# r of tiles 0 to 11 loaded in runs of eight tokens and turned by 64x64 transposes; rstd on ScalarE; a new order for all engines

## The chip, the cores and the metric

The kernel runs on one core of one Trainium2 chip. The engines of the core are TensorE (PE in the profile), VectorE (DVE), ScalarE (ACT), GpSimd (POOL) and SyncE (SP, which here only issues transfers). The metric is the device time of one execution in microseconds (us). The kernel before has a median of 148.78 us over three runs (147.83, 148.78 and 149.36).

## The reference

There are 4 batches, 8 heads, 768 tokens and 48 channels for each head. The first half is a linear recurrence of attention with a decay w for each head and channel, the second half is a feed-forward block on the 384 channels of a token.

```
state = 0                                            # per batch and head, 48 x 48
for t in range(768):
    cur = u * k[t] (outer) v[t]
    y[t] = r[t] @ (state + cur)
    state = w * state + k[t] (outer) v[t]

x  = y as (batch, token, 8 heads * 48 = 384)
xn = (x - mean(x)) / sqrt(var(x) + 1e-6) * g_ln
out = x + relu(xn @ w_ch1) @ w_ch2                   # 384 -> 1536 -> 384
```

All inputs and the output are in float32.

## The kernel before

**Tiles.** The 768 tokens of a batch are cut into 6 chunks of 128. A tile i is chunk i // 4 of batch i % 4, so there are 24 tiles of 128 tokens, and tile i needs the state that tile i - 4 leaves. Within a tile the recurrence becomes matrix products. With powers of w folded in, r is multiplied by w^t (`Fr`) and k by w^-(t+1) (`Fk`), t being the token's place in the chunk, which is its partition.

**Steps of one tile.** `LR`, `LK`, `LV` load r, k and v as [128 tokens, 8 heads, 48], so that every run in memory is 48 floats, 192 bytes. `SR` and `SK` scale r and k and write them in bf16 to `sc`, each head padded to 64 columns. `TR` turns r and k on TensorE with 128x128 transposes (line 348), two heads at a time, and `TCr`, `TCk` (or `TC` for both) copy the result from PSUM to `trs`. For tiles 12 to 23 (`K_BY_DMA`) a transposing transfer, `TKR`, does this instead. `AT` (line 371) makes the token-by-token products k r of all heads, from 48 rows of the array at row 0 or row 64; `AM` (or `AMa` and `AMb`) masks them into `A`. `Q` multiplies turned r and k; `S` sums that with u and w to the coefficient of a token's own v (line 402), copied by `CC` to `cc`, and makes the new state (lines 409 and 415), which `ZU` and `ZD` decay and keep as `Z`. `VB` forms cc * v, `Y` (lines 444 and 452) makes r state + A v, and `X` adds them to x and gives the row sum. `SQ` and `XN` centre x and sum its squares, `RS` makes the reciprocal of the standard deviation, `LT` (line 512) and `XT` turn the centred x, or `LT2` and `LTD` do so by a transfer.

**Feed-forward.** Tiles are taken in 17 groups of one or two (`GROUPS`). `UP` (line 527) multiplies by w_ch1 (12 matmuls of 128 or 6 of 256 columns), `RL` applies relu on the way out of PSUM, `DN` (line 557) multiplies by w_ch2 (4 matmuls of 384 columns), `OT` scales by `rs` and adds x, `STO` stores. For a group of one tile, `UP` number m needs third m of w_ch1. The weights come in thirds: `LW1` loads a third (768 KB), `SW` scales it by the layer norm's gain and rounds it to bf16 in three pieces; `LW2` and `CW` do the same for w_ch2. The last tile is finished in two halves (`DA`, `DB`, `OA`, `OB`, `SA`, `SB`).

**Order.** There is no planner in the kernel: the string `PLAN` lists some 800 steps as name, number and engine or PSUM bank ("v" VectorE, "s" ScalarE, "g" GpSimd; "h", "p", "o", "a" banks), and each step issues its instructions at once. Every engine works through its own instructions in that order, and a transfer marked "-" is issued by SP in that order too. `DU` issues matmuls on zeros while the first loads are under way.

The steps that matter most for what follows:

```
def chunk_src(t, i):
    c, b = divmod(i, B)
    return t[b, :, c * L : (c + 1) * L, :].rearrange("h t d -> t h d")
def LR(i, e):
    nc.sync.dma_start(out=rf(i)[:], in_=chunk_src(r, i))
def SR(i, e):
    times(e, scr(i)[:, :, :D], rf(i)[:], Fr[:])
```

Of the kernel before, what the change touches and what calls it, by code (L numbers as in the profile page):

```python
# [9 lines left out]
ALU = mybir.AluOpType  # L10
# [8 lines left out]
LR,1,- LK,0,- MI,0,g MW,0,v WF,0,s WB,0,- LC,0,s LC,1,s MM,0,g MP,0,v TL,0,s LC,2,s DU,21,h LN,0,s FK,0,s FR,0,s SK,0,v LK,1,- LR,0,- SK,1,v CT,0,o  # L19
DU,7,h SR,0,v TR,0,h TCk,0,s SR,1,v TR,1,h TCk,1,v TCr,0,s Q,0,v AT,0,- CP,0,s WL,0,s LR,2,- SR,2,g TCr,1,v LK,2,- SK,2,g TR,2,h AMb,0,v AMa,0,v  # L20
AT,1,- LV,1,- LK,3,- AMb,1,v AMa,1,v UW,0,g TCk,2,s TCr,2,s AT,2,- AMb,2,v UGC,0,s LV,0,- CV,0,s S,0,h CC,0,v VB,0,v ZU,0,v Y,0,h X,0,v XN,0,v LR,3,-
CV,1,s Q,1,g SK,3,g SR,3,g TR,3,- Q,2,g S,1,o CC,1,v VB,1,g ZU,1,v AMa,2,v Y,1,- X,1,v LK,5,- LR,4,- SR,4,g TCr,3,s TCk,3,s AT,3,- Q,3,v AM,3,v LV,2,-
CV,2,s S,2,h CC,2,s ZU,2,v LT,0,o XN,1,s XT,0,s LK,4,- LR,5,- SR,5,v VB,2,v SK,4,g DU,3,p TR,4,- TC,4,v Q,4,v LV,3,- CV,3,s S,3,o CC,3,s SQ,1,s ZU,3,v
LV,4,- SK,5,g TR,5,- TC,5,s VB,3,g Y,2,- X,2,v LT,1,- XT,1,s XN,2,s CV,4,g S,4,h ZU,4,v CC,4,s LV,5,- CV,5,g ATP,4,- AM,4,v LW1,0,- SW,1,s Y,3,h
SQ,0,s X,3,v XN,3,s SQ,2,s LT,2,h XT,2,v Q,5,g S,5,- AM,5,v ZU,5,v Y,4,o SW,2,g SW,0,g UP,16,- RL,16,s LW1,2,- SW,6,s CC,5,s LT,3,- XT,3,s UP,32,-
RL,32,s UP,0,- RL,0,s LW1,1,- SW,5,s VB,4,g X,4,v XN,4,v SW,7,g SW,8,g UP,2,o RL,2,v VB,5,g UP,48,p RL,48,v Y,5,h SW,3,g LK,6,- SK,6,v X,5,v UP,18,-
RL,18,s XN,5,s SW,4,g UP,49,p RL,49,s UP,33,o LR,7,- SR,7,v UP,34,- RL,34,s LK,7,- SK,7,g RS,2,g RL,33,v UP,17,- RL,17,s TR,7,p TC,7,s RS,0,g LT,5,h
XT,5,v LT,4,- UP,1,o LR,6,- Q,7,v LW2,2,- UP,82,- SR,6,g TR,6,- UP,81,- XT,4,s RL,1,v LV,7,- CV,7,v CW,5,v S,7,- CC,7,v ZU,7,v CW,4,g DN,6,- RL,82,v
TC,6,s Q,6,g ATP,6,- AM,7,v AM,6,v LW2,1,- CW,2,s SQ,4,s DN,2,p UP,50,- RL,50,s CW,3,g DN,5,- VB,7,g DN,1,- RL,81,v Y,7,h LW2,0,- CW,1,s CW,0,g DN,4,-
DN,0,- SQ,5,s RS,1,g OT,1,v LV,6,- CV,6,s S,6,h CC,6,s LK,9,- SK,9,g UP,66,o SQ,3,s X,7,v XN,7,g SQ,7,s VB,6,g ZU,6,v RL,66,v UP,64,- RL,64,s Y,6,h  # L30
LR,9,- SR,9,v LR,8,- SR,8,g DN,10,- RS,5,g TR,9,- X,6,v XN,6,s LK,8,- SK,8,v DN,8,- OT,0,v TR,8,- TC,8,v Q,8,v TC,9,s Q,9,v RS,3,g RS,4,g DN,9,-
OT,2,v UP,65,- RL,65,s ATP,8,- UP,80,p AM,9,v LV,9,- CV,9,g LR,10,- SR,10,g DN,18,- S,9,h ZU,9,v DN,17,- CC,9,v LK,10,- SK,10,g LV,8,- CV,8,s S,8,h
LR,11,- SR,11,v CC,8,v RL,80,s ZU,8,v VB,9,g TR,10,- AM,8,v TC,10,v VB,8,g LT2,6,- UP,96,- RL,96,s Q,10,v UP,98,p RL,98,s UP,97,- RL,97,s Y,9,h X,9,v
LK,11,- UP,100,p RL,100,s LV,10,- LR,15,- LK,12,- SK,11,g TR,11,- TC,11,s XN,9,v CV,10,g S,10,h Y,8,h X,8,v XN,8,s ZD,8,g DN,16,- ATP,10,- STO,0,-
OT,4,v UP,101,- RL,101,s UP,99,p LR,13,- SK,12,g SQ,6,s RL,99,s STO,1,- DN,22,- DN,20,- DN,21,- ZU,10,v AM,10,v DN,14,p CC,10,v DN,12,- Q,11,g ZD,10,v
SR,13,g LV,11,- CV,11,s S,11,h CC,11,s AM,11,v OT,5,v Y,10,h VB,10,v X,10,v ZD,9,g ZU,11,v LR,12,- SR,12,g LK,13,- SK,13,g LR,14,- SR,14,v VB,11,g
# [12 lines left out]
DN,49,- LV,19,- CV,19,s CC,18,s S,19,h ZU,19,v DN,42,- ZD,18,g VB,18,g STO,8,- OT,12,v CC,19,s Y,18,h X,18,v LT2,16,- UP,176,- RL,176,s LR,21,-
UP,178,o RL,178,s XN,18,s UP,181,- RL,181,s AM,19,v Y,19,h VB,19,v X,19,v XN,19,s DN,62,- DN,61,- DN,60,- LR,20,- STO,6,- OT,10,v LK,20,- LR,22,-  # L50
SR,22,v SQ,17,s DN,57,p UP,179,- RL,179,s RS,10,g UP,177,- RL,177,v STO,11,- DN,56,- UP,180,- SQ,16,s RL,180,s SR,21,g TKR,21,- Q,21,v OT,15,v DN,58,-
S,21,o CC,21,s LT2,18,- UP,194,- RL,194,s STO,10,- OT,14,v UP,196,- RL,196,v UP,192,p SK,20,g LK,22,- SK,22,v SQ,18,s UP,193,- RL,193,s UP,195,-
RL,195,s SR,20,g TKR,20,- Q,20,v ATP,20,- AM,20,v S,20,h DN,65,- DN,64,- ZD,19,g RL,192,s LV,20,- CV,20,s Y,20,h CC,20,v VB,20,v SQ,19,s X,20,v
# [11 lines left out]
def kernel(  # L65
# [262 lines left out]
    def LR(i, e):  # L328
        nc.sync.dma_start(out=rf(i)[:], in_=chunk_src(r, i))  # L329
# [333 lines left out]
```

## Time and profile before

| | |
|---|---|
| median of 3 runs | 148.78 us (147.83 to 149.36) |
| profiled execution: time, span from first to last instruction | 148.24 us, 146.5 us |
| mean granted TensorE clock | 0.965 |
| busy PE, DVE, ACT, POOL | 135.8, 110.5, 80.1, 94.0 us |
| DMA packets, and those under 512 bytes | 99267, 94508 |
| HBM read and written | 18.88 MB, 4.72 MB |

The busy times are sums over the whole span; they say little by themselves, since the span has a front in which the loads come in and the first tiles are prepared, a long middle in which the feed-forward runs, and an end. The rows of single stretches, the order of the instructions in time and the chain that ended last are shown where they are used.

### The profile page before, as it was taken

What the parts mean: (1) busy time and instruction counts of PE and PEld (TensorE: products, weight loads), DVE (VectorE), ACT (ScalarE), POOL (GpSimd) and SP (SyncE); (2) the same over time, 40 slices, a digit from 0 to 9 for tenths busy, and PEclk for the clock granted to TensorE, in tenths of its full rate; (3) what the DMA queues carried; (4) which work ended last, traced back from release to release, by engine and by line L of the source; (5) the groups of instructions that cost most, each with busy time, mean ns of one, the idle gap of its engine ahead of it and who ended that gap; (6) DMA issues with size and microseconds to landing.
All of it is one profiled execution on the core that took longest, in us unless ns stands there. A gap on an engine that the chain in (4) does not pass through costs nothing.

```text
span 146.5 us, 4250 instructions
## 1 busy us (share of the span) xinstructions
PE 135.8 (93%) x1693; PEld 108.2 (74%) x1693; DVE 110.5 (75%) x220; ACT 80.1 (55%) x175; POOL 94.0 (64%) x132
## 2 busy tenths in 40 slices
PE   3966699999999999999999999999999999999991
PEld 1455477998687897787688887966877777888871
DVE  4569999767969899985959948897946796875232
ACT  2575577977676467466386560663654752244600
POOL 4089878967888999989957493428553076644030
PEclk9999556999999999999999999999999999999999
DMA  5999899999889999899999999988999997830114
GB/s 97 209 211 221 175 277 401 194 258 380 231 170 188 206 197 232 156 215 242 96 229 206 260 233 186 217 166 185 245 157 199 229 184 156 206 123 0 54 37 182
DMA packets 99267, 28.59 MB, mean 195 GB/s; under 512 B 94508, under 2 KB 97712, under 8 KB 99248
## 3 DMA queue, kind: packets, MB, share of 16 engines
q1 hardware_dynamic: 98352, 27.24, 86.3%
q10 hardware_dynamic: 896, 1.09, 2.0%
q8 instruction: 13, 0.21, 0.6%
q14 instruction: 6, 0.05, 0.1%
HBM read 18.88 MB, written 4.72 MB: 161 GB/s over the span
## 4 chain that ended last, share of the span: by engine, by line
PE 60%; SPq 11%; DMA 11%; DVE 7%; POOL 6%; issue 4%; DVEq 0%; POOLq 0%
PE hp L527 17%; PE o L557 16%; PE s L557 7%; PE s L527 5%; SPq L332 4%; DMA w_f<-in_moe_w_ch_dram 4%; SPq L329 4%; SPq L326 3%; DMA trs<-sc 3%; DMA rf<-in_r_dram 3%; PE o L527 3%; PE at L371 2%; PE hp L452 2%; POOL sc L194 2%; PE at L348 2%
## 5 line engine op out<-in xcount | busy, mean ns | idle before, releaser
L527 PEld LDWEIGHTS <-w_sb 128*128 128x128 bf16 x612 | 47.9, 114 | 2.4 <-POOL w_sb L312 0.4
L527 PE MATMUL hp<-xT,w_sb 128*128 128x128 bf16 (+1 forms) x408 | 39.9, 244 | 0.3 <-POOL w_sb L312 0.3
L557 PEld LDWEIGHTS <-hT 128*128 128x128 bf16 x276 | 25.2, 97 | 13.7 <-issue 0.4
L557 PE MATMUL o<-w_sb,hT 128*128 128x384 bf16 x180 | 34.5, 326 | 0.0
L543 ACT ACTIVATE hT<-hp 128x512 bf16<-128x512 f32 x41 | 24.3, 597 | 18.2 <-PE hp L527 17.7
L381 DVE TENSOR_TENSOR A<-at,mask 128x1024 bf16<-128x1024 f32 (+1 forms) x27 | 28.9, 1096 | 1.2 <-PE at L371 1.2
L194 POOL TENSOR_TENSOR sc<-kf,Fk 128x384 bf16<-128x384 f32 x14 | 14.5, 1044 | 10.5 <-DMA kf<-in_k_dram 10.4
L434 POOL TENSOR_TENSOR Vb<-vf,cc 128x384 f32<-128x384 f32 x17 | 14.7, 868 | 8.7 <-ACT cc L189 3.6
L557 PE MATMUL s<-w_sb,hT 128*128 128x384 bf16 x96 | 18.9, 326 | 0.2 <-DVE x L459 0.2
L194 POOL TENSOR_TENSOR q<-trs 128x512 bf16<-128x512 bf16 x11 | 13.4, 1220 | 5.5 <-PE hp L527 2.6
L194 POOL TENSOR_TENSOR sc<-rf,Fr 128x384 bf16<-128x384 f32 x12 | 13.0, 1082 | 5.3 <-DMA rf<-in_r_dram 5.3
L466 ACT ACTIVATE sqj<-x,sm 128x384 bf16<-128x384 f32 x24 | 14.7, 611 | 1.4 <-DVE x L459 1.3
L615 DVE SCALAR_TENSOR_TENSOR ot<-o,rs,x 128x384 f32<-128x384 f32 x15 | 9.2, 613 | 4.5 <-POOL rs L483 2.8
L459 DVE SCALAR_TENSOR_TENSOR x<-hp,Vb 128x384 f32<-128x384 f32 x19 | 10.5, 554 | 2.3 <-PE hp L452 1.6
L483 POOL TENSOR_TENSOR rs<-rs,expo 128x1 f32<-128x1 f32 (+1 forms) x17 | 10.6, 625 | 1.4
L472 ACT ACTIVATE xn<-x,sm 128x384 bf16<-128x384 f32 x13 | 8.0, 613 | 5.7 <-DVE x L459 5.6
L371 PE MATMUL at<-trs 48*128 48x128 bf16 x192 | 8.6, 229 | 2.4 <-ACT trs L189 1.2
L527 PE MATMUL s<-xT,w_sb 128*128 128x128 bf16 (+1 forms) x120 | 10.8, 235 | 0.0
L194 POOL TENSOR_TENSOR Z<-ZS,WLZ 128x384 bf16<-128x384 f32 x10 | 10.3, 1030 | 0.6 <-DVE ZS L428 0.6
L545 DVE TENSOR_SCALAR hT<-hp 128x512 bf16<-128x512 f32 x9 | 6.2, 689 | 4.6 <-PE hp L527 4.6
L371 PEld LDWEIGHTS <-trs 48*128 48x128 bf16 x192 | 6.0, 99 | 4.9 <-ACT trs L189 2.1
L194 DVE TENSOR_TENSOR sc<-rf,Fr 128x384 bf16<-128x384 f32 x12 | 7.5, 633 | 2.3 <-DMA rf<-in_r_dram 2.2
(116 smaller groups left out, 214.3 us busy)
## 6 DMA issues: line engine op xcount, KB each, us to landing
rf<-in_r_dram SPq DMA_DIRECT2D x24, 192.0 KB, 3.8
kf<-in_k_dram SPq DMA_DIRECT2D x24, 192.0 KB, 3.9
vf<-in_v_dram SPq DMA_DIRECT2D x24, 192.0 KB, 3.9
w_f<-in_moe_w_ch_dram SPq DMA_DIRECT2D x6, 768.0 KB, 7.2
out_dram<-ot SPq DMA_DIRECT2D x18, 192.0 KB, 3.4
out_dram<-ot ACTq DMA_DIRECT2D x5, 192.0 KB, 2.0
trs<-sc SPq DMA_TRANSPOSE x12, 3.9
xT<-xn SPq DMA_TRANSPOSE x9, 2.8
```

What stands on the lines that cost most here:

```text
L194: engines[e].tensor_tensor(out=out, in0=in0, in1=in1, op=ALU.mult)
L371: nc.tensor.matmul(out=t[:, par, q, :], lhsT=trs(i)[p0 : p0 + D, 1, q, :], rhs=trs(i)[p0 : p0 + D, 0, q, :], start=True, stop=True,)
L381: nc.vector.tensor_tensor(out=AA(i)[:, a:b].rearrange("p e q t -> p (e q) t"), in0=psum["at", i][:, a:b].rearrange("p e q t -> p (e q) t") ...
L434: engines[e].tensor_tensor(out=Vb(i)[:].rearrange("p (h d) -> p h d", h=H), in0=vf(i)[:], in1=cc(i)[:].unsqueeze(2).to_broadcast([P, H, D] ...
L459: nc.vector.scalar_tensor_tensor(out=xx(i)[:], in0=psum["y", i][:, :C], scalar=1.0, in1=Vb(i)[:], op0=ALU.mult, op1=ALU.add, accum_out=sm[ ...
L466: nc.scalar.activation(out=sqj[:], in_=xx(i)[:], func=ACT.Square, bias=sm[i][:], scale=-float(C), accum_out=sq[g][:, j : j + 1])
L472: nc.scalar.activation(out=xn(i), in_=xx(i)[:], func=ACT.Identity, bias=sm[i][:], scale=-float(C))
L483: nc.gpsimd.tensor_tensor(out=rs[g][:], in0=rs[g][:], in1=expo[:, :n], op=ALU.pow)
L527: nc.tensor.matmul(out=t[:, a * gw : (a + 1) * gw].rearrange("p (j t) -> p j t", j=size), lhsT=w1_sb[n][kc][:, fb::FB], rhs=xT(g)[:, :size ...
L543: nc.scalar.activation(out=o, in_=s, func=ACT.Relu)
L557: nc.tensor.matmul(out=psum["o", i][:, :C], lhsT=hT(g)[:, fk, j * P : (j + 1) * P], rhs=w2_sb[d][:, a, :], start=(seen == 0 and a == 0), s ...
L615: nc.vector.scalar_tensor_tensor(out=ot(i), in0=psum["o", i][:, :C], scalar=rs[g][:, j : j + 1], in1=xx(i)[:], op0=ALU.mult, op1=ALU.add,)
```

## The change

**r of tiles 0 to 11.** `LR` no longer puts one token on each partition. Partition 16 h + p holds tokens 8 p to 8 p + 7 of head h, one run of 8 x 48 floats (1536 bytes). The power of w then depends on the head and on the place in the run, so there is a second table, `Fq`, with its own short preparation: `MR` and `MU` make the token numbers, `MS` a selection matrix, `WS` two matmuls that spread w over the partitions, `LNQ` their logarithm, `FA` the product, `FQ` the exponential. `Fr` is needed only from tile 12 on, is made later and shares its memory with the logarithms of `Fk`. `TR` turns r of these tiles with 16 transposes of 64x64 (eight places in the run, two halves of the partitions) in place of four of 128x128; k keeps its four. `TCr` writes the result with a stride of 8 so that tokens come in order. `TC`, which copied r and k together, is not used any more.

**Pairs of heads.** Since the lower half of the partitions now holds heads 0 to 3 and the upper half heads 4 to 7, the pairs of heads are (q, q + 4) and no longer (2q, 2q + 1). `SK`, `SR`, `CV`, `CC`, `LC` and `Y` put that order into their access patterns.

**rstd.** `RS` was two instructions on GpSimd, the second a power of -0.5. It is now a logarithm and an exponential on ScalarE, from the same activation table that the kernel loads already.

**VB** can also run on ScalarE, as 8 instructions of 48 columns; 3 of the 24 do.

**Order, engines and banks** are all set anew. Of the loads, the first third of w_ch1 now stands behind 18 loads of 192 KB, of which 7 are packed r, as before it stood behind 18 loads, all in runs of 192 bytes; the thirds of w_ch1 are no longer issued in a row, but with one k load, and then a k and an r load, between them. The steps before the first `UP` are nearly the same set: `S` of tile 5 and `Y` of tile 4 now come behind it.

```diff
+PACK = 8
+R_PACKED = 12
-... WB,0,- ... DU,21,h LN,0,s FK,0,s FR,0,s SK,0,v ... LV,3,- ... LV,4,- ... LV,5,- ... LW1,0,- SW,1,s ... LW1,2,- ... LW1,1,- ...
+LK,2,- LR,2,- LK,0,- MW,0,v MM,0,g WF,0,s LC,2,s WB,0,h LC,0,s TL,0,s MI,0,g MS,0,v WS,0,o LC,1,s LN,0,s MR,0,g MU,0,v MP,0,v FK,0,s SK,0,v DU,19,h
+LNQ,0,s FA,0,v FQ,0,s CT,0,o CP,0,s UGC,0,s UW,0,g SK,2,v LR,0,- SR,0,v TR,0,p TCr,0,s ...
+X,1,v ATP,4,- AM,5,v LW1,2,- SW,8,s SW,7,s XN,2,g LT,2,p XT,2,s XN,1,s SW,6,g UP,50,- RL,50,s LK,7,- SK,7,g LW1,0,- ...
...
-    expo = const.tile([P, GM], FP32, name="expo")
+    eps = const.tile([P, 1], FP32, name="eps")
-    ln_all = const.tile([P, H, D], FP32, name="ln_all")
+    ln_all = Fr
...
+    def WS(i, e):
+        t = psum["wq"] = bank(e, "p", [P, 512], FP32)
+        for a in range(2):
+            nc.tensor.matmul(
+                out=t[:, :D], lhsT=sel[:, 2 * a : 2 * a + 2, :].rearrange("k e x -> k (e x)"),
+                rhs=rows[:HP, a * DP : a * DP + D], start=(a == 0), stop=(a == 1),
+            )
+
+    def LNQ(i, e):
+        nc.scalar.activation(out=lnq[:], in_=psum["wq"][:, :D], func=ACT.Ln)
+
+    def FA(i, e):
+        times(
+            e, Fq[:], lnq[:].unsqueeze(1).to_broadcast([P, PACK, D]),
+            pow_r[:].unsqueeze(2).to_broadcast([P, PACK, D]),
+        )
+
+    def FQ(i, e):
+        nc.scalar.activation(out=Fq[:], in_=Fq[:], func=ACT.Exp)
...
     def LR(i, e):
-        nc.sync.dma_start(out=rf(i)[:], in_=chunk_src(r, i))
+        if i >= R_PACKED:
+            issuer(e).dma_start(out=rf(i)[:], in_=chunk_src(r, i))
+            return
+        c, b = divmod(i, B)
+        issuer(e).dma_start(
+            out=rf(i)[:].rearrange("p j d -> p (j d)"),
+            in_=r[b, :, c * L : (c + 1) * L, :].rearrange("h (p j) d -> h p (j d)", j=PACK),
+        )
...
     def SK(i, e):
-        times(e, sck(i)[:, :, :D], kf(i)[:], Fk[:])
+        times(e, paired(sck(i))[:, :, :, :D], plain(kf(i)[:]), plain(Fk[:]))
...
     def TR(i, e):
...
+        to = t[:, :HP, :].rearrange("p q (a t) -> p (q a) t", a=2)
+        for j in range(PACK):
+            for par in range(2):
+                part = slice(par * DP, (par + 1) * DP)
+                nc.tensor.transpose(out=to[part, j, :], in_=scr(i)[part, j, :], identity=ident[part, part])
 
     def TCr(i, e):
-        copy(e, trs(i)[:, 0], psum["tr", i][:, :HP])
+        if i < R_PACKED:
+            copy(
+                e, trs(i)[:, 0].rearrange("p q (t j) -> p j q t", j=PACK),
+                psum["tr", i][:, :HP, :].rearrange("p a (b q t) -> p (a b) q t", b=2, q=HP),
+            )
+        else:
+            copy(e, trs(i)[:, 0], psum["tr", i][:, :HP])
...
     def RS(g, e):
-        n = GROUPS[g]
-        nc.gpsimd.tensor_scalar(
-            out=rs[g][:], in0=sq[g][:], scalar1=1.0 / C, scalar2=1e-6 * C * C, op0=ALU.mult, op1=ALU.add
-        )
-        nc.gpsimd.tensor_tensor(out=rs[g][:], in0=rs[g][:], in1=expo[:, :n], op=ALU.pow)
+        nc.scalar.activation(out=rs[g][:], in_=sq[g][:], func=ACT.Ln, bias=eps[:], scale=1.0 / C)
+        nc.scalar.activation(out=rs[g][:], in_=rs[g][:], func=ACT.Exp, scale=-0.5)
```

More of the change, by code (lines that the diff above doesn't have):

```diff
@@ L21 @@
[L21 to L24, printed above, removed]
@@ L93 @@
     FB = FW // P
+    LP = L // PACK
+    assert H == PACK and H * LP == P
     assert D <= DP and H % 2 == 0 and S % L == 0 and C % P == 0 and F % (P * NW) == 0
```

148 lines of the change are left out of this document (94 added, 54 removed).

## The prediction

> **What bounds the kernel now.** I read the page first, then the stretches, then the chain of work that ended last, then single instructions in time. The page says that TensorE is busy nearly throughout, that its clock is halved for a while early on, and that the DMA engines are loaded to over nine tenths almost to the end.
>
> ```profile
> span 146.5 us, 4250 instructions
> PE   3966699999999999999999999999999999999991
> PEclk9999556999999999999999999999999999999999
> DMA  5999899999889999899999999988999997830114
> ```
>
> A busy TensorE need not be at its peak, so the next view is the stretches (first two columns the stretch and its length, then busy time of PE, weight loads, DVE, ACT, POOL, then clock, DMA share, GB/s).
>
> ```profile
> 2.00:18.00 16.00, 12.15 (x128) 7.66 (x128) 11.65 (x28) 9.69 (x21) 9.97 (x12) 0.87 1.03 204
> 9.10:25.10 16.00, 12.44 (x187) 9.87 (x186) 15.81 (x34) 10.55 (x27) 13.83 (x18) 0.68 1.00 255
> 14.00:24.00 10.00, 8.58 (x111) 6.66 (x109) 9.84 (x22) 6.41 (x15) 8.05 (x10) 0.50 0.95 259
> 20.00:24.00 4.00, 4.00 (x59) 3.21 (x57) 3.88 (x9) 2.94 (x7) 3.35 (x5) 0.50 1.01 374
> 25.10:143.50 118.40, 117.31 (x1477) 95.34 (x1477) 90.25 (x170) 65.52 (x143) 77.11 (x102) 1.00 0.89 191
> 143.50:146.50 3.00, 0.00 (x0) 0.00 (x0) 0.42 (x1) 0.00 (x0) 0.00 (x0) 1.00 0.37 137
> ```
>
> From 25.10 to 143.50 TensorE is busy for 117.31 of 118.40 us at full clock, while DVE has 28, POOL 41 and ACT 53 us to spare. The chain in that stretch is matmul behind matmul:
>
> ```profile
> 36.00 0.08 PE s L402 x4
> 36.08 0.18 PE s L409
> 36.26 0.17 PE s L415 x4
> ...
> 37.08 0.55 PE at L371 x16
> 37.63 0.76 PE s L557 x4
> ...
> 43.95 0.17 PE hp L444 x4
> 44.12 0.20 PE hp L452 x8
> 44.32 0.65 PE o L557 x4
> 44.97 0.45 PE at L348 x8
> 45.42 0.65 PE o L557 x4
> ```
>
> So the middle is bound by the number and size of matmuls, and the time is: when the first `UP` can start, plus the TensorE work left from there, plus 3.0 us for the last half tile's add and store, plus 148.24 - 146.5 = 1.74 us outside the span. What sets the first `UP` is the load of w_ch1 and its scaling:
>
> ```profile
> 5.19 0.60 ACT L280 ACTIVATE Fr<-ln_all,pow_i 128x384 f32<-128x384 f32 x1
> 13.72 3.96 SPq L332 DMA_DIRECT2D vf<-in_v_dram  x3
> 17.72 1.71 SPq L301 DMA_DIRECT2D w_f<-in_moe_w_ch_dram  x3
> 23.65 0.72 ACT L308 ACTIVATE w_sb<-w_f,g_neg 128x512 bf16<-128x512 f32 x1 [0.78 <-DMA w_f<-in_moe_w_ch_dram]
> 23.67 1.37 POOL L312 TENSOR_SCALAR w_sb<-w_f,g_neg 128x512 bf16<-128x512 f32 x2 [0.66 <-DMA w_f<-in_moe_w_ch_dram]
> 25.10 0.86 PE L527 MATMUL hp<-xT,w_sb 128*128 128x128 bf16 x12 [0.27 <-POOL w_sb L312]
> ```
>
> ACT and POOL idle until the weights land at 23.65, and the slower of the two, POOL with two pieces in a row, lets TensorE go at 25.10. Ahead of the weights the DMA engines are full (share 1.03) with 18 loads.
>
> **Part by part: the loads.** A load is 192 KB, 196608 bytes: at the 204 GB/s of the stretch 2 to 18, which holds nothing but 192-byte runs, it takes 0.96 us; at the 374 GB/s of 20 to 24, which is w_ch1 in 2 KB runs, 0.53 us. One single microsecond of that goes at 412 GB/s:
>
> ```profile
> 23.00:24.00 1.00, 1.00 (x18) 0.84 (x17) 1.00 (x2) 0.35 (x1) 0.34 (x2) 0.50 1.06 412
> ```
>
> That is 0.48 us a load. Runs of 1536 bytes are not in the loads of before; 2 KB is the nearest row, so a packed r saves 0.43 to 0.48 us. Seven stand ahead of w_ch1: 3.0 to 3.4 us, taken as 3.2. Scaling stays as long: two ACT pieces in a row (2 x 0.72) in place of two on POOL (1.37); while `SW` 8 waits for the weights on ACT, `SW` 7, `XT` 2, `XN` 1 and the first `RL` queue behind it, and all but the first are due only for that `UP` or later. The first `UP` would so start at 25.1 - 3.2 = 21.9. Before, three thirds of w_ch1 were issued in one go and the first landed about 5.9 us after its issue; with one k load behind it, it could land sooner by up to (786432 bytes at 374 GB/s = 2.1 us, less the 0.96 of that k load) 1.1 us, or not at all. I take 0, since nothing in the trace shows a third landing faster. The five other packed tiles come after the first `UP`; a DMA engine that is less full is worth nothing there while TensorE waits for 1.09 us in all.
>
> **64x64 transposes.** Per tile, four of the eight transposes of line 348 (0.45 us for 8, so 0.225 for 4) become 16 of half the columns. The nearest row by size is line 452: 8 matmuls of 48 columns in 0.20 us, 25 ns each, and 16 x 25 = 0.40 us. The nearest row that uses half the array's rows is line 371, 16 in 0.55, or 34 ns each; and the four `DN` matmuls behind it take 0.76 us where others take 0.65, so a change of the array's layout and back costs 0.11. I take 0.40 + 0.11 - 0.225 = 0.29 us a tile. From below: if the two halves of the array work at the same time, as line 371 suggests (128 columns in 34 ns, where line 348 needs 56), 16 take 0.22 and the tile pays just 0.11; a cost of 0 would need the change of layout to vanish also. From above stands the weight load of a small operand, not hidden at all:
>
> ```profile
> L452 PEld LDWEIGHTS <-A 128*128 128x128 bf16 x192 | 7.5, 99 | 0.4 <-issue 0.2
> ```
>
> 16 x 0.099 = 1.58 us, +1.47 a tile. Six tiles (6 to 11) are turned behind the first `UP`: 6 x 0.29 = 1.74 us, with ends 0 and 8.8. The other six fall into the front, three of them (4, 1, 5) in the stretch at half clock, where TensorE had 10.00 - 8.58 = 1.42 us free; 3 x 0.29 x 2 = 1.74 nearly fits.
>
> The rule that speaks against this part is in the Trainium skill, "TensorEngine Tiling (Array Packing)", sections Key Properties and Restrictions: changing the tiling mode drains TensorE, and column tiling switches fast weight load off. The 0.76 against 0.65 us agrees with the drain; no matmul of before tiles columns, so the second half is open here. With the rate that "TensorE: Matmul & The Clock Gate", section LDWEIGHTS, gives without fast load (columns / 1.2 ns, so 53 ns for 64 columns) an estimate is 0.85 us for 16, +0.74 a tile and 4.4 us for six in place of my 1.74, and the sum below would be 150.2.
>
> **Work moved behind the first UP.** `S` of tile 5 (0.08 + 0.18 + 0.17) and `Y` of tile 4 (0.17 + 0.20): 0.80 us.
>
> **rstd.**
>
> ```profile
> L483 POOL TENSOR_TENSOR rs<-rs,expo 128x1 f32<-128x1 f32 x10 | 5.6, 559 | 0.8
> L483 POOL TENSOR_TENSOR rs<-rs,expo 128x2 f32<-128x2 f32 x7 | 5.0, 721 | 0.6
> L291 ACT ACTIVATE ln_p<-cols 128x4 f32<-128x4 f32 x1 | 0.2, 205 | 0.0
> L543 ACT ACTIVATE hT<-hp 128x512 bf16<-128x512 f32 x41 | 24.3, 597 | 18.2 <-PE hp L527 17.7
> ```
>
> POOL loses at least 10.6 us, ACT gains 34 x 0.205 = 7.0. Neither is the bound: ACT's relu alone waits 17.7 us for TensorE, and that cover hides the 7 us; without it each `RS` would hold the next relu, and so a PSUM bank, for 0.41 us. Counted as 0, also for `OT`, which is off TensorE's path unless it keeps a bank. The same cover takes `VB` on ACT (8 small instructions, about 8 x 0.2 us, three times) and the separate `TCr` and `TCk`; the strided access of `SK`, `CV`, `TCr` has no row, and 0.2 us on each of 60 such steps would be 12 us over three engines that have 122 to spare.
>
> **The front's own chain.** `Fr` was ready at 5.8. `Fq` comes after `Fk`, `LNQ`, `FA` on DVE and `FQ` on ACT, some 0.2 + 0.5 + 0.6 us later, and the first `SR` waits for it; DVE has one more `SK` to do meanwhile. Counted as 0, up to 1 us if it isn't hidden. The last store changes from the second to the first column half: 0.
>
> **Sum.** 148.24 - 3.2 + 0.80 + 1.74 = 147.6 us. This stands against the profiled execution, which lies 0.5 us under the median of 148.78 and within its runs; I leave it at 147.6.
>
> **Rivals.** *The front gives more and the transposes cost little* (R1): w_ch1's first third lands 1.1 us sooner, and the 64x64 transposes pair up at 0.11 a tile: 148.24 - 3.2 - 1.1 + 0.80 + 0.66 = 145.4. For it: line 371's pace, and a stream of matmuls that was interrupted for 1.09 us at most. Against it: 14 to 24 at half clock, which an `UP` at 21 would run into.
>
> *VectorE sets the front* (R3): in 9.10 to 25.10 DVE is busy for 15.81 of 16.00 us, so weights that come earlier may find x not ready. What DVE has to do ahead of the first `UP` changes by these rows:
>
> ```profile
> L381 DVE TENSOR_TENSOR A<-at,mask 128x1024 bf16<-128x1024 f32 x21 | 25.1, 1216 | 1.2 <-PE at L371 1.2
> L191 DVE COPY trs<-at 128x1024 bf16<-128x1024 bf16 x3 | 2.0, 682 | 0.1
> L434 DVE TENSOR_TENSOR Vb<-vf,cc 128x384 f32<-128x384 f32 x7 | 4.8, 687 | 0.3 <-ACT cc L189 0.2
> L474 DVE TENSOR_SCALAR xn<-x,sm 128x384 bf16<-128x384 f32 x8 | 4.2, 532 | 0.2
> L194 DVE TENSOR_TENSOR Z<-hp,WLZ 128x384 bf16<-128x384 f32 x4 | 2.2, 552 | 0.3 <-ACT cc L189 0.2
> L194 DVE TENSOR_TENSOR sc<-kf,Fk 128x384 bf16<-128x384 f32 x10 | 5.7, 584 | 3.0 <-ACT Fk L277 3.0
> L194 DVE TENSOR_TENSOR sc<-rf,Fr 128x384 bf16<-128x384 f32 x12 | 7.5, 633 | 2.3 <-DMA rf<-in_r_dram 2.2
> ```
>
> By the order, one `AM` (1.22), one `TC` (0.68), two `VB` (1.37), one `XN` (0.53) and one `ZU` (0.55) go to a later place or another engine, 4.4 us; two `SK` (1.17), one `SR` (0.63) and `FA` (priced as an `SK`, 0.58) come, 2.4 us. So DVE is done 2.0 sooner, the first `UP` starts no earlier than that, and the time is 148.24 - 2.0 + 0.80 + 1.74 = 148.8, no change.
>
> *Slower* (R2): the weight load of a 64x64 transpose isn't hidden behind the one before it. If two halves of the array load side by side, 16 take 8 x 0.099 = 0.79 us, +0.68 a tile and 4.1 us behind the first `UP`. In the half-clocked stretch three tiles add 3 x 0.68 x 2 = 4.1 us to a TensorE with 1.42 to spare, and the 3.2 us of the front shrink to 0.5. That gives 148.24 - 3.2 + 0.80 + 4.1 = 149.9 if the front keeps its gain, and 152.6 if not; 151.2 between. It decides from (3.2 - 0.8) / 6 = 0.40 us a tile, which is 32 ns a transpose: less than line 371's own 34. The Trainium skill adds, in "TensorE: Matmul & The Clock Gate", section PE-mode transpose, that transposes do not count as activity for the clock in the way of other matmuls; by that rule they would not lift the half clock of 14 to 24, and the 152.6 would be the end to take. No row of before can tell.
>
> **Chances.** Forecast (146.4 to 148.6) 0.36, R1 0.31, R3 0.14, R2 0.19. The sum is 147.6; the range 144.8 to 150.8 leaves out the lower end of R1, where the 1.09 us of waits go too, and the upper part of R2. A measurement here tells 1% from no change, 147.3 and 150.3 against the median: faster is R1 and a third of the forecast, 0.43; slower is R2, 0.19; the rest is 0.38.
>
> **What would show it.** The first matmul of line `UP` at about 22 us, with the weight scaling that frees it waiting for a DMA (if it waits for DVE or for TensorE, R3 or the clock is right). In the chain, 16 transposes in 0.4 us and a longer matmul group behind them; 0.8 us or more is R2, 0.2 R1. TensorE busy for all but about 1 us from the first `UP` to the end, with the time for that stretch 118.4 + 2.5 = 120.9 us. Packed loads at 374 GB/s or more; POOL's busy time down, ACT's up by 7 us. A wait of TensorE on ACT behind `RS`, or for the later thirds of w_ch1, would make the forecast wrong in a way that none of the cases has.

## The result and the profile after

The changed kernel takes 161.87 us (median of 4 runs, 161.37 to 162.43) against 148.44 us of the kernel before on the same chip. The ratio is 1.09, with a 95% interval of 1.0828 to 1.0972: 9% slower, where 147.6 us was forecast in a range of 144.8 to 150.8. Its profiled execution has a span of 160.2 us. Medians here and below are over all runs of a kernel, ratios over those in the chip's fast state alone.

The page, then the stretches (columns as in the prediction) of the changed kernel:

```profile
span 160.2 us, 4582 instructions
PE   4939447698899997799999999999999999999992
ACT  3278999988997479969378887415404361164620
PEclk9999999999999999999999999999999999999998
PE 59%; ACT 18%; DVE 11%; DMA 6%; SPq 3%; issue 2%; POOL 0%; DVEq 0%; ACTq 0%
...
10.00:20.00 10.00, 6.08 (x104) 4.38 (x103) 6.09 (x13) 9.48 (x7) 3.77 (x5) 1.00 0.91 189
20.00:30.00 10.00, 6.05 (x97) 5.04 (x97) 6.72 (x17) 9.69 (x24) 6.45 (x8) 1.00 1.07 306
```

From 10 to 30 us ScalarE is busy for 19.17 of 20 us and TensorE for 12.13; before, in the 16 us up to the first `UP`, ScalarE was busy for 10.55 and TensorE for 12.44. The fifth line is the summary of the chain that ended last: ScalarE, which had no share in the chain before, has 18% of it. The chain in the front shows what ScalarE is doing, and the next fence, the first matmul of `UP`:

```profile
12.65 5.21 ACT trs L199 x3
...
17.87 2.28 ACT trs L199
...
25.58 2.76 ACT trs L199 x2
...
29.12 2.84 ACT trs L199 x2
```

```profile
32.84 1.45 PE L608 MATMUL hp<-xT,w_sb 128*128 128x128 bf16 x11
```

`trs` is what `TCr` and `TCk` write, from PSUM, where the matmuls leave their results, to SBUF, where the tiles stand. The rows of that tile (duration in ns, shortest, median and longest) hold both kinds of copy:

```profile
L199 ACT COPY trs<-at x7: 565/2457/2787, 15.1 to 62.7; 128x512 bf16<-128x512 bf16 x7
L201 DVE COPY trs<-at x5: 411/425/2479, 17.9 to 61.6; 128x512 bf16<-128x512 bf16 x5
```

The shortest are `TCk`, which writes in order: 0.57 us on ScalarE, 0.41 on VectorE. The longest are `TCr`, which writes each element 8 places behind the one before it: 2.3 to 2.8 us on ScalarE, 2.4 to 2.5 on VectorE. Six of the twelve stand ahead of the first `UP`, all on ScalarE. After it they go on, in the same chain, on VectorE too:

```profile
54.04 2.39 DVE trs L201
```

So the first `UP` moved from 25.10 to 32.84 us instead of to 21.9, and the stretch from there to the last matmul grew from 118.37 to 124.44 us, where 120.9 was forecast.

### The profile page after: what moved, and what is told of

The parts are those of the page before. It is cut to its first block, busy times and chain, and to the rows that moved or that the text cites. A ratio compares the mean times of both kernels' runs of the same rounds, so it can differ in the third digit from the quotient of the medians.

```text
span 160.2 us, 4582 instructions
## 1 busy us (share of the span) xinstructions
PE 142.1 (89%) x1835; PEld 113.9 (71%) x1835; DVE 122.2 (76%) x234; ACT 100.7 (63%) x224; POOL 81.7 (51%) x106
## 3 DMA queue, kind: packets, MB, share of 16 engines
q10 hardware_dynamic: 896, 1.09, 1.8%
## 4 chain that ended last, share of the span: by engine, by line
PE 59%; ACT 18%; DVE 11%; DMA 6%; SPq 3%; issue 2%; POOL 0%; DVEq 0%; ACTq 0%
PE hp L608 17%; PE o L638 13%; ACT trs L199 12%; PE s L638 9%; PE s L608 5%; DMA rf<-in_r_dram 4%; DVE trs L201 3%; PE at L449 3%; DMA vf<-in_v_dram 2%; ACT Vb L518 2%; PE o L608 2%; SPq L370 2%; PE hp L536 1%; DVE sc L204 1%; ACT hT L624 1%
## 5 line engine op out<-in xcount | busy, mean ns | idle before, releaser
L624 ACT ACTIVATE hT<-hp 128x512 bf16<-128x512 f32 x35 | 20.6, 604 | 20.8 <-PE hp L608 17.9
L638 PE MATMUL o<-w_sb,hT 128*128 128x384 bf16 x168 | 32.0, 326 | 0.0
L638 PE MATMUL s<-w_sb,hT 128*128 128x384 bf16 x108 | 21.0, 327 | 0.0
L558 POOL TENSOR_SCALAR xn<-x,sm 128x384 bf16<-128x384 f32 x11 | 7.2, 653 | 18.5 <-DVE x L543 18.5
L204 POOL TENSOR_TENSOR q<-trs 128x512 bf16<-128x512 bf16 x9 | 10.6, 1175 | 6.4 <-ACT trs L199 4.7
L201 POOL CAST vv<-vf 128x384 bf16<-128x384 f32 x12 | 6.5, 546 | 13.0 <-DMA vf<-in_v_dram 13.0
L626 DVE TENSOR_SCALAR hT<-hp 128x512 bf16<-128x512 f32 x16 | 11.0, 687 | 2.7 <-PE hp L608 2.0
L204 POOL TENSOR_TENSOR sc<-rf,Fr 128x384 bf16<-128x384 f32 x9 | 9.6, 1070 | 5.5 <-DMA rf<-in_r_dram 5.5
L199 ACT COPY trs<-at 128x512 bf16<-128x512 bf16 x7 | 11.8, 1707 | 0.5 <-PE at L420 0.5
L204 DVE TENSOR_TENSOR sc<-kf,Fk 128x384 bf16<-128x384 f32 x10 | 7.4, 739 | 3.2 <-DMA kf<-in_k_dram 3.2
```

Of the source, the lines that this page charges most:

```text
L199: nc.scalar.copy(out=out, in_=in_)
L201: engines[e].tensor_copy(out=out, in_=in_)
L204: engines[e].tensor_tensor(out=out, in0=in0, in1=in1, op=ALU.mult)
L624: nc.scalar.activation(out=o, in_=s, func=ACT.Relu)
L626: nc.vector.tensor_relu(out=o, in_=s)
L638: nc.tensor.matmul(out=psum["o", i][:, :C], lhsT=hT(g)[:, fk, j * P : (j + 1) * P], rhs=w2_sb[d][:, a, :], start=(seen == 0 and a == 0), s ...
```

## The experiments

**The copy.** The suspect is the strided write of `TCr`. First, a copy that goes straight through (tokens then in the wrong order):

```diff
-            copy(e, trs(i)[:, 0].rearrange("p q (t j) -> p j q t", j=PACK),
-                psum["tr", i][:, :HP, :].rearrange("p a (b q t) -> p (a b) q t", b=2, q=HP))
+            copy(e, trs(i)[:, 0], psum["tr", i][:, :HP])
```

> The changed kernel with one thing taken away: the copy of turned r (TCr) of tiles 0 to 11 writes its 512 elements side by side and no longer with a stride of 8 elements. r of these tiles so stands in the order in which the transposes leave it, not in the order of the tokens; nothing else is left out or moved. Theory S (the strided copy is the cause: 12 copies of about 2.4 us, nine on ACT and three on DVE, in place of 0.42 to 0.59): the copies fall to 0.6 (ACT) and 0.42 (DVE) and the time to that of the blind sum, 145 to 150 us. Rival T (the new order, the 64x64 transposes and RS on ACT cost the time by themselves): above 155 us. Between 150 and 155 both have a share.

151.67 us, ratio 1.0235 (1.0170 to 1.0301): between S and T, so that the copy is most of the loss and the rest of the change has a share. Second, the same tokens in the right order, with the stride moved from the write to the read:

```diff
-                e, trs(i)[:, 0].rearrange("p q (t j) -> p j q t", j=PACK),
-                psum["tr", i][:, :HP, :].rearrange("p a (b q t) -> p (a b) q t", b=2, q=HP),
+                e, trs(i)[:, 0].rearrange("p q (t j) -> p q t j", j=PACK),
+                psum["tr", i][:, :HP, :].rearrange("p a (b q t) -> p q t (a b)", b=2, q=HP),
```

> The same elements moved by the same twelve copies to the same places, in another order: the write runs side by side and the read from PSUM jumps by 64 elements each time. Theory S, with the price on the write into SBUF alone: copies of 0.4 to 0.7 us and the time of the run with the contiguous copy, 145 to 150 us. If a jump costs on the reading side just as much: copies of about 2.4 us and 160 us or more. If PSUM reads are dearer but less so: copies of 1 to 1.5 us and 150 to 156.

152.09 us, ratio 1.0229 (1.0120 to 1.0338): the copies are as cheap as S said, and the time is that of the run before, over S's 150. The largest of its groups of such copies (both kinds in it):

```profile
L199 ACT COPY trs<-at 128x512 bf16<-128x512 bf16 x7 | 4.0, 586 | 0.5 <-PE at L420 0.5
```

On ScalarE the read with jumps of 128 bytes in PSUM costs nothing; the write with jumps of 16 bytes in SBUF cost some 1.85 us a copy more. Third, the strided write alone, put into the kernel before (tokens in the wrong order; `TC` split into `TCr` and `TCk`):

```diff
     def TCr(i, e):
-        copy(e, trs(i)[:, 0], psum["tr", i][:, :HP])
+        copy(e, trs(i)[:, 0].rearrange("p q (t j) -> p j q t", j=8),
+            psum["tr", i][:, :HP, :].rearrange("p a (b q t) -> p (a b) q t", b=2, q=HP))
```

> The kernel before with one thing added: the copy of turned r of every tile that is turned on TensorE writes with a stride of 8 elements (r of these tiles then stands in a wrong order of tokens), and where r and k were copied together they are copied one after the other. Theory S: twelve copies of about 2.4 us, and a time of 155 to 163 us, about what the change as a whole costs. Rival T: the copies are slow, but beside other work, and the time stays within 148 to 152 us.

162.26 us, ratio 1.0903 (1.0800 to 1.1005). Put into the kernel before, this copy pattern costs as much as the whole change; taken out of the changed kernel, it leaves 2.3%. Together that is more than the 9% of the change, so the parts do not simply add up; how they overlap is not shown. The split of `TC`, one more copy in eight tiles, is part of this run and was not tried alone.

**The stride by itself.** Copies of 512 bf16 elements for each partition behind the end of the kernel before, in one execution (code shortened):

```diff
+            act(out=by(o, n), in_=seq(flat, n))     # writes n elements apart: 1, 2, 4, 8, 16, 64
+            act(out=seq(f, n), in_=by(flat, n))     # reads n apart in PSUM: 2, 8, 64
+            act(out=seq(f, n), in_=by(o, n))        # reads n apart in SBUF: 2, 8, 64; then all on VectorE
```

> The kernel before, and behind its last store twelve copies of 512 bf16 elements a partition on ScalarE and then the same twelve on VectorE: from PSUM to SBUF with writes 1, 2, 4, 8, 16 and 64 elements apart; with reads 2, 8 and 64 apart in PSUM and contiguous writes; and with reads 2, 8 and 64 apart in SBUF. Theory S: the price is that of a write that begins a new 16 bytes each time, so writes 1, 2 and 4 apart take near 0.6 us on ScalarE, those 8 and more apart take 2.3 to 2.5 us, on both engines alike, and no read costs more than 0.8 us. Rival G (the price grows with the stride step by step): 2 and 4 apart take 1 and 1.7 us, 64 apart more than 2.5. Rival R (reads in SBUF pay as writes do): reads 8 apart in SBUF take 2 us or more.

Instructions in order of time (start, duration); ScalarE's writes 1, 2, 4, 8, 16 and 64 apart are L635 to L640, VectorE's first four L648 to L651, its reads 2 and 8 apart in PSUM L654 and L655:

```profile
143.99 0.59 ACT L635 COPY trs<-at 128x512 bf16<-128x512 bf16 x1 [5.58 <-DMA out_dram<-ot]
144.61 0.73 ACT L636 COPY trs<-at 128x512 bf16<-128x512 bf16 x1
145.37 1.29 ACT L637 COPY trs<-at 128x512 bf16<-128x512 bf16 x1
146.69 2.42 ACT L638 COPY trs<-at 128x512 bf16<-128x512 bf16 x1
149.14 2.29 ACT L639 COPY trs<-at 128x512 bf16<-128x512 bf16 x1
151.47 2.43 ACT L640 COPY trs<-at 128x512 bf16<-128x512 bf16 x1
...
158.51 0.41 DVE L648 COPY trs<-at 128x512 bf16<-128x512 bf16 x1
158.96 0.72 DVE L649 COPY trs<-at 128x512 bf16<-128x512 bf16 x1
159.72 1.29 DVE L650 COPY trs<-at 128x512 bf16<-128x512 bf16 x1
161.04 2.42 DVE L651 COPY trs<-at 128x512 bf16<-128x512 bf16 x1
...
167.88 0.89 DVE L654 COPY A<-at 128x512 bf16<-128x512 bf16 x1
168.81 0.69 DVE L655 COPY A<-at 128x512 bf16<-128x512 bf16 x1
```

Neither S nor G is right as written: the time nearly doubles with each doubling of the stride from 2 to 8 elements and then stays. Counted in steps to a new 16 bytes (128, 256, 512, 512, 512) it is 4.5 to 5.7 ns a step, the same on both engines. R falls: no read took more than 1.09 us, though S had none over 0.8. The Trainium skill states this limit in "SBUF — State Buffer", section Specifications: lines of 16 bytes, and a penalty for each access that goes to a new one; the trace agrees, and adds the price. It does not agree that two hits in a line are enough, as four elements apart (two hits) take 1.29 us where in order they take 0.59 and 0.41.

**Packing, taken apart.** The changed kernel with r loaded and turned as before (`Fr` is made early again):

```diff
-R_PACKED = 12
+R_PACKED = 0
-... MS,0,v WS,0,o LC,1,s LN,0,s MR,0,g MU,0,v MP,0,v ... LNQ,0,s FA,0,v FQ,0,s CT,0,o ...
+... LC,1,s LN,0,s MP,0,v ... FR,0,s CT,0,o ...
```

> The changed kernel with r of tiles 0 to 11 loaded and turned as before (192-byte runs, four 128x128 transposes, contiguous copy), and Fr made early in the place of the second table; order, engines, banks, pairs of heads and RS as changed. Theory S: without the strided copy the time falls to 146 to 152 us, the first UP some 3 us later than with packed r and contiguous copies, since w_ch1 stands behind 18 slow loads again. Rival T (the new order costs the time): above 155 us.

149.5 us, ratio 1.0126 (1.0078 to 1.0174), inside S's range. But the first `UP` came at 24.92 us, not 3 us later than with packed r and the copy in order (26.88) but 2 us sooner. So packing does not pay even with a cheap copy, and order, rstd and `VB` together cost the 1.3% that are left. Then each part alone in the kernel before, the loads first:

```diff
-        nc.sync.dma_start(out=rf(i)[:], in_=chunk_src(r, i))
+        nc.sync.dma_start(out=rf(i)[:].rearrange("p j d -> p (j d)"),    # for i < 12
+            in_=r[b, :, c * L : (c + 1) * L, :].rearrange("h (p j) d -> h p (j d)", j=8))
```

> The kernel before, with one edit: r of tiles 0 to 11 is loaded in runs of 8 tokens per head. Nothing else is changed, so the tokens of r stand in a wrong order in these tiles (order left out). Theory L (a packed load takes 0.48 to 0.53 us of the DMA engines, as the prediction priced it): seven of them stand ahead of w_ch1, the first UP moves from 25.1 to about 21.9 us, the kernel gets 2 to 3.2 us faster, 145 to 146.5. Theory M (in the front the 1536-byte packets share the engines badly with the 192-byte ones: 0.7 us and more a load and engines idle a fifth of the time, as the kernels with packed r and a contiguous copy showed it): w_ch1 is issued no sooner, the first UP is at 24.5 to 27 and the time 148 to 150. Between 22.5 and 24.5 each has a part.

148.92 us, ratio 1.0029 (0.9990 to 1.0069): no gain. SP's queue shows the load of w_ch1, issued at 17.72 us before, and the next row the first `UP`, at 25.10 before:

```profile
16.12 2.88 SPq L339 DMA_DIRECT2D vf<-in_v_dram  x3
19.04 1.83 SPq L301 DMA_DIRECT2D w_f<-in_moe_w_ch_dram  x3
```

```profile
27.71 1.11 PE L534 MATMUL hp<-xT,w_sb 128*128 128x128 bf16 x12
```

The packed loads make the front longer, as M said, and by more (it had 24.5 to 27). But the first `UP` 2.6 us later cost 0.8 us of span in this execution, and in the medians no difference clear of noise, so in this order the front isn't worth what the prediction paid for it either. rstd on ScalarE alone:

```diff
-        nc.gpsimd.tensor_scalar(out=rs[g][:], in0=sq[g][:], scalar1=1.0 / C, ...)
-        nc.gpsimd.tensor_tensor(out=rs[g][:], in0=rs[g][:], in1=expo[:, :n], op=ALU.pow)
+        nc.scalar.activation(out=rs[g][:], in_=sq[g][:], func=ACT.Ln, bias=eps[:], scale=1.0 / C)
+        nc.scalar.activation(out=rs[g][:], in_=rs[g][:], func=ACT.Exp, scale=-0.5)
```

> The kernel before, with one edit: rstd (RS) as Ln and Exp on ScalarE in place of the two steps on POOL. Theory S (it is hidden by ScalarE's idle time, as predicted): 147.5 to 148.5, within 0.4% of before; ScalarE's busy time up by 7 to 8.5 us, POOL's down by 10 or more. Theory A (each RS holds the next relu and with it a PSUM bank for 0.4 to 0.6 us, which costs TensorE a part): 149 to 151.

150.66 us, ratio 1.0151 (1.0109 to 1.0192): A's time. A piece of its chain shows the path that the prediction had counted as hidden:

```profile
68.92 0.50 ACT hT L540
69.42 0.19 ACT rs L479
69.64 0.21 ACT rs L480
69.87 0.62 DVE ot L612
70.49 1.14 DVE A L381
71.68 0.38 PE hp L452 x8
```

`RS` queues behind a relu, `OT` on VectorE waits for `RS`, the mask behind `OT` on VectorE waits too, and TensorE waits for the mask. It waits for `ot` directly as well, since `OT` keeps a PSUM bank (a piece of PSUM that one step fills and another must empty). So the price comes by way of `OT` and VectorE, not by the next relu as A had it:

```profile
PE o L524 <- DVE ot L612: 0.7, 1, 0.7
PE hp L452 <- DVE A L381: 0.5, 1, 0.5
PE o L402 <- DVE ot L612: 0.5, 1, 0.5
```

Last, the 64x64 transposes alone (16 for four, loads and copies as before, r wrongly placed):

```diff
+        for j in range(8):
+            for par in range(2):
+                nc.tensor.transpose(out=to[part, j, :], in_=scr(i)[part, j, :], identity=ident[part, part])
```

> The kernel before, with one edit: r of tiles 0 to 11 is turned by sixteen 64x64 transposes in place of four 128x128 ones; loads, copies and order as before (r stands in a wrong order in its transpose, order left out). Theory P (a 64x64 transpose takes 23 to 25 ns, as predicted): +0.15 to 0.3 us a tile, six tiles behind the first UP, +0.9 to 1.8 us, and up to as much in the front: 149 to 151. Rival W (weight loads not hidden, 0.68 us a tile): 152 or more. Rival H (hidden by TensorE's waits in the front, and cheap behind it): under 148.7.

150.4 us, ratio 1.0115 (1.0045 to 1.0185), inside P's range. The chain gives 0.37 us for 16 and 0.22 for four, 0.15 a tile more:

```profile
45.82 0.22 PE at L347 x4
46.04 0.37 PE at L352 x16
```

From the first `UP` to the last matmul TensorE is busy for 118.30 us where it was 117.31 before, 0.99 more for the six tiles. The rest of the 1.7 us is not work on TensorE; this execution waits 1.6 us at one place for POOL's `vv`.

**rstd in the order made for ScalarE.** The run with r not packed, with `RS` on POOL again (the diff of rstd above, reversed):

> The changed kernel's order with r not packed, as in the run before with r not packed (149.5 us), and rstd in two steps on POOL again. Theory S (in the new order ScalarE's idle time hides rstd): 149 to 150.5, the same within 0.5%. Theory A (rstd on ScalarE costs about 2 us in any order, as it did in the old one): 147 to 148. Rival P (the new order leaves POOL no room): over 151.

156.74 us, ratio 1.0585 (1.0495 to 1.0674). P holds: TensorE now waits for POOL's other work, 1.9 us for `vv` and 1.7 us for `sc` at one place each. So the share of rstd in the 1.3% can't be found by putting it back; it stays open.

**What the first `UP` is worth.** The kernel before with w_ch1 one load sooner:

```diff
-LV,5,- CV,5,g ATP,4,- AM,4,v LW1,0,- SW,1,s ... Q,5,g S,5,- AM,5,v ZU,5,v Y,4,o SW,2,g SW,0,g UP,16,- RL,16,s
+LW1,0,- LV,5,- ATP,4,- AM,4,v SW,1,s ... Q,5,g AM,5,v Y,4,o SW,2,g SW,0,g UP,16,- RL,16,s CV,5,g S,5,- ZU,5,v
```

> The kernel before with w_ch1's first third issued one load sooner, ahead of v of tile 5, and the steps that need that v (its cast, S and the state of tile 5) behind the first UP. Theory F (the first UP sets the time, as the prediction had it: it moves from 25.1 to about 23.7, and 0.4 us of work with it behind): 147.4 to 148. Theory N (the first UP's time is worth little, since TensorE then waits for other things; packed loads alone moved it 2.6 us later for 0.4 us of time): 148.2 to 149.2.

148.73 us, ratio 1.0001 (0.9955 to 1.0046), as N had it. The load is issued 2.3 us sooner than before. The scaling starts behind POOL's own work, with no wait for the load, and the first `UP` still starts at 25.05 us, with no wait for the scaling:

```profile
15.42 1.63 SPq L301 DMA_DIRECT2D w_f<-in_moe_w_ch_dram  x1
...
23.38 1.37 POOL L312 TENSOR_SCALAR w_sb<-w_f,g_neg 128x512 bf16<-128x512 f32 x2
...
25.05 1.27 PE L527 MATMUL hp<-xT,w_sb 128*128 128x128 bf16 x12
```

The chain that ended last runs over VectorE's queue up to 21.73 us here, and from there over TensorE's own matmuls up to `UP`; with packed loads alone it is the same, up to 23.80. In the changed kernel with the strided read, too, the scaling starts with no wait for the load, at 24.25 us, and `UP` with no wait for the scaling, at 26.78. What a load more than one place sooner would do was not tried.

**Why the packed loads were slow.** Groups of ten loads behind the end of the kernel before, each group alone. This run and the two that follow are one execution each:

> The kernel before, and behind its last store three groups of ten loads of 192 KB, each group starting when the one before has landed: ten in 192-byte runs, ten packed in 1536-byte runs, and five of each in turn. Theory D (the packed load is slow wherever it runs, as a 1536-byte read takes 70 ns or more): the second group takes 7 us or more for its ten, and the third lies halfway. Theory M (it is slow only where it shares the engines with 192-byte packets): 9 to 10.5 us for the first group, 5 to 6 for the second, and the third no better than the first, 9 us or more, with engines idle part of the time. Theory O (neither; packed loads cost what the prediction said and the front was slow for another reason): the third takes 7 to 8 us.

In 192-byte runs one load landed in 0.90 us (first to last, 147.04 to 155.18 us, over 9), packed in 1.08 us (159.25 to 169.01), in turn in 1.10 us. The second group takes D's time, the third M's, as it does not lie halfway. D's reason fails: in the packed group the DMA engines' share is about 0.53, and the median packet takes 65 ns, so that 128 of them are 0.52 us of 16 engines, as the prediction had it. Half of what the engines could do goes unused, with no 192-byte packet beside. Next, three orders of the same 1536-byte runs (code shortened):

```diff
+   in_=rows_of(j).rearrange("h (p j) d -> h p (j d)", j=8)                          # as in the change
+   in_=r.rearrange("b h s d -> (b h s d)").rearrange("(n p x) -> n p x", p=P, x=8 * D)[j]
+   in_=rows_of(j)[a * HP : (a + 1) * HP].rearrange("h (p j) d -> p h (j d)", j=8)   # two halves
```

> The kernel before, and behind its last store three groups of loads of r, 1536-byte runs in all three, each group starting when the one before has landed: ten as in the change (8 heads, and in each 16 runs); ten of 128 runs that follow each other in memory; ten in two halves of 4 heads with the tokens as the outer order (16 token groups, and in each 4 heads). Theory E (the DMA engines are dealt out by the outer order of a load, and 8 heads reach only 8 of 16): the first group lands one load a us at a share of about 0.53, as in the run of loads by themselves, the second and third one in 0.5 to 0.65 us at a share near 1. Rival B (memory gives no more for these runs): all three at about 1 us and 180 to 200 GB/s. Rival H (8 heads far apart are slow, in whatever order): the second is fast, the third is not.

1.02, 0.66 and 1.32 us a load. The third can't tell E from H, as SP took 13.09 us for its 20 issues. So once more, the third group in one load per tile:

> As the run on the order of a load by itself, but the third group takes each tile in one load of 128 partitions with the tokens as the outer order (16 token groups, and in each 8 heads), so that SP issues it once and not twice. First and second group as there: one load in 1.02 us at a share of 0.53, and in 0.66 us. Theory E (a load is dealt out to the DMA engines by its outer order, and an outer order of 8 reaches 8 engines): the third lands one load in 0.5 to 0.7 us at a share of 0.8 or more, as the 8 heads are no longer the outer order; the halves before were held by SP's issue, 20 times 0.65 us. Rival H (8 heads far apart in memory are slow in any order): 1 us or more a load at a share near 0.5.

Stretches inside each group, then the first and the last landing of the first and of the third group (tiles `kf` and `vf`):

```profile
148.00:156.00 8.00, 0.00 (x0) 0.00 (x0) 1.09 (x7) 0.00 (x0) 0.00 (x0) 0.51 0.51 188
160.00:164.00 4.00, 0.00 (x0) 0.00 (x0) 0.84 (x6) 0.00 (x0) 0.00 (x0) 0.50 0.93 278
170.00:176.00 6.00, 0.00 (x0) 0.00 (x0) 0.94 (x6) 0.00 (x0) 0.00 (x0) 0.50 0.94 274
```

```profile
148.51 0.16 DVE L643 CAST sqj<-kf 128x1 bf16<-128x1 f32 x1 [2.14 <-DMA kf<-in_r_dram]
...
158.19 0.16 DVE L643 CAST sqj<-kf 128x1 bf16<-128x1 f32 x1 [0.83 <-DMA kf<-in_r_dram]
...
171.11 0.16 DVE L643 CAST sqj<-vf 128x1 bf16<-128x1 f32 x1 [1.63 <-DMA vf<-in_r_dram]
...
177.70 0.16 DVE L643 CAST sqj<-vf 128x1 bf16<-128x1 f32 x1 [0.32 <-DMA vf<-in_r_dram]
```

The same heads and runs with 16 token groups outermost use the engines at a share of 0.94, not 0.51, and land in 0.73 us, not 1.08: a little over E's 0.7, while H falls. The packets of the trace bear E out: in the first stretch 7 to 9 of them are under way for 0.89 of the time, in the third 13 to 18 for 0.88, and the median one takes 65 ns in both. The Trainium skill states the rule in "DMA: Bandwidth & Descriptors", section "Why a DMA increments its semaphore by 16 and not by 1": the number of engines is the largest, up to 16, that divides the slowest dimension of both sides, here 8 and 128, so 8. The trace agrees.

**With the loads mended.** The changed kernel with the strided read, r in two halves with the tokens outermost (`Fq`'s selection and the copy's read follow):

```diff
+            for a in range(2):
+                issuer(e).dma_start(out=rf(i)[a * DP : (a + 1) * DP].rearrange("p j d -> p (j d)"),
+                    in_=r[b, a * HP : (a + 1) * HP, c * L : (c + 1) * L, :].rearrange("h (p j) d -> p h (j d)", j=PACK))
```

> The changed kernel with a contiguous write in the copy (as in the run with a strided read, 152.1 us), and r loaded in two halves of 4 heads with the tokens as the outer order; the selection for Fq and the read of the copy follow that order. Theory E with the first UP as the bound: the front gains what the packed loads were to give, first UP at 23.5 to 25, 149 to 150.5 us. Rival N (the loads get faster, but the first UP waits for other work, as it did where w_ch1 was issued one load sooner): first UP at 25 to 26.5, 150.5 to 152. Rival D (twice the number of r loads holds the queue of SP): 152 or more.

152.14 us, ratio 1.0260 (1.0160 to 1.0360). The first `UP` came at 25.09 us, 1.7 sooner than with the strided read alone, and the time stayed. The first `UP` is in N's range, the time in D's, and the trace bears D out. SP issues w_ch1 1.1 us later than with the strided read alone (first row, against the second), and its queue has 27% of the chain that ended last, where it had 3%:

```profile
18.17 0.58 SPq L350 DMA_DIRECT2D w_f<-in_moe_w_ch_dram  x1
...
17.09 1.59 SPq L345 DMA_DIRECT2D w_f<-in_moe_w_ch_dram  x1
...
PE 37%; SPq 27%; DMA 14%; DVE 9%; issue 4%; ACT 4%; POOL 3%; DVEq 0%; ACTq 0%; POOLq 0%
```

So this run does not show what faster r loads are worth without more of them; one load with the tokens outermost for all 8 heads was not tried in the kernel. The stretches from the first `UP` to the last matmul, of the kernel before, of packed loads alone, r not packed, the strided read, and this one:

```profile
25.10:143.47 118.37, 117.31 (x1477) 95.34 (x1477) 90.25 (x170) 65.52 (x143) 77.11 (x102) 1.00 0.89 191
```

```profile
27.71:144.28 116.57, 116.27 (x1482) 95.44 (x1478) 88.78 (x170) 65.10 (x142) 75.64 (x101) 1.00 0.89 190
```

```profile
24.92:144.48 119.56, 118.07 (x1500) 97.27 (x1498) 93.74 (x180) 69.21 (x185) 67.16 (x78) 1.00 0.89 191
```

```profile
26.78:146.96 120.18, 119.47 (x1572) 97.91 (x1570) 97.31 (x180) 69.78 (x186) 67.11 (x78) 1.00 0.86 187
```

```profile
25.09:147.42 122.33, 119.25 (x1570) 97.46 (x1570) 94.34 (x180) 70.34 (x187) 67.77 (x78) 1.00 0.88 188
```

Stretch less TensorE's busy time is 1.06, 0.30, 1.49, 0.71 and 3.08 us: in both pairs with the same order of work (second against first row, fifth against fourth) the front that ends sooner has more waits behind it. In the fifth SP's queue may be a cause as well, so this is not shown as a rule. No version here beats the kernel before.

## Why the prediction was wrong

By spans the 13.7 us split so, each step the difference of two single profiled executions (the end behind the last matmul is 0.1 us shorter):

| step | kernels compared | first `UP` | stretch behind it |
|---|---|---|---|
| strided write | changed, against strided read | +6.06 | +4.26 |
| packed loads and 64x64 transposes | strided read, against r not packed | +1.86 | +0.62 |
| order, rstd, `VB`, the moved steps | r not packed, against before | -0.18 | +1.19 |

- **"The strided access of SK, CV, TCr has no row, and 0.2 us on each of 60 such steps would be 12 us over three engines that have 122 to spare."** This step failed, and it is the main one: 10.3 of the 13.7 us by the table, 9% in the order of before. Of the three it names, only `TCr` cost anything: `SK` takes 0.55 us on VectorE and `CV` 0.51 on ScalarE, as before. `TCr` cost 1.85 us and more a copy, nine times the bound. And the 122 us to spare were a sum over the stretch from 25.10 us on, while six of the copies stand ahead of it, on ScalarE, with `Q` and TensorE behind them. The range took in no price for it at all.
- **"What sets the first UP is the load of w_ch1 and its scaling."** This failed too. The row that was quoted gave the sign: TensorE had waited only 0.27 us for POOL, so its own queue was nearly as late. With w_ch1 issued 2.3 us sooner, the work on VectorE and TensorE held the first `UP` at 25.05 us. So the -3.2 us was not to be had in that order by the load of w_ch1 alone. R3, in which VectorE sets the front, was nearer, though its 2.0 us sooner was also too much: 0.18 with r not packed.
- **The packed load at 0.48 to 0.53 us.** The time of its packets was right, its landing wrong by a factor of two (1.08 us), as only half the engines take part. So the seven packed loads ahead of w_ch1 saved nothing: SP issued it at 17.80 us, before at 17.72.
- **64x64 transposes, 0.40 us for 16 and 0.29 a tile.** 0.37 measured, and 0.15 a tile, as nothing shows the 0.11 for a change of layout. That the part alone cost 1.7 us in the medians, where the sum had 1.74, is luck: TensorE's work grew by 0.99 us, the rest is waits. R2 falls: a transpose takes 23 ns, under its 32. The estimate of 0.85 us that the prediction drew from the Trainium skill was more than twice too high. The granted clock was 0.997 or more in every run of the changed kernel, so the second rule it drew on, that transposes would leave the half clock in place, had nothing to act on there. With the 64x64 transposes alone the half clock lasted 6.8 us, against 10.2 before: no sign of it either. What brings the half clock about is open.
- **0.80 us for S and Y moved behind the first UP.** The stretch with r not packed is 1.19 us longer, and TensorE is busy for 0.76 us more in it (118.07 against 117.31), near the 0.80. The other 0.43 us is waits, in which rstd's part was not told apart.
- **rstd at 0.** This failed as well, in the order of before: 8.3 us on ScalarE, 7.0 forecast, and alone it cost 2.2 us. The clause "unless it keeps a bank" was the case, and `OT` held the mask behind it on VectorE besides.
- **`Fq`'s chain, 0 to 1 us.** `Fq` was ready at 8.37 us, 2.6 later than `Fr` before, not 1.3. The chain that ended last does not pass it: it comes from an r load that landed at 11.33 us. So it shows no cost here.
- **VB on ScalarE, 8 x 0.2 us.** 1.91 us for eight, where 1.6 was taken. It stands in the chain that ended last twice, at 23.27 and at 92.50 us, so it was not covered; what it cost was not tried alone.

## What to carry to other kernels

Before a copy is called free, write down the distance in bytes between its successive writes. Turn the loops so that the write runs in order and put the jumps on the read from PSUM. Before a transfer is priced by the rate of its packets, look at its outermost dimension. Before work is moved ahead, check that what it frees really waited for it: the bracket behind the first dependent instruction says by how much. Idle time of an engine hides new work only in the stretch, and behind the queue, where that work will stand.

## What the runs showed of the hardware

In copies of 512 bf16 elements from PSUM, a write that steps to a new 16 bytes of SBUF each time takes 4.5 to 4.7 ns an element on ScalarE and on VectorE alike. Reads are cheaper: in PSUM 8 or 64 elements apart 0.59 us on ScalarE (0.59 in order) and 0.69 on VectorE (0.41 in order), but 2 apart 0.92 and 0.89, more than 8 apart, for which I have no explanation. From SBUF, 8 or 64 apart took 1.09 and 1.05 us on ScalarE, 0.61 and 0.59 on VectorE. A load of 192 KB in runs of 1536 bytes whose outermost dimension is 8 ran at 188 GB/s, where the same bytes with 16 outermost ran at 274. Moving rstd between engines cost time in both directions, 1.5% in an order made for POOL, and 4.5% (1.0585 over 1.0126) in one made for ScalarE.
